# Attention and a mixture of experts on one core: the experts' second product with tokens as the stationary side

## The chip, the cores and the metric

The kernel runs on one core of a Trainium2 chip. The metric is device microseconds of one execution. TensorE (PE in the profile, PEld for its weight loads) multiplies a stationary operand of up to 128 columns with a moving operand and writes PSUM; VectorE (DVE) and ScalarE (ACT) read PSUM and copy; GpSimd (POOL) issues the gathers and scatters; SyncE (SP) issues the weight loads.

## The reference

Attention of 4 batches, 8 heads, 576 tokens, 64 features with a position bias; its output, as 2304 rows of 512, goes through eight experts, one per token:

```
logits = x @ w_gate;  e_idx = argmax(logits)
gate_w = softmax(logits)[e_idx];  eom = sigmoid(x @ w_output_gate)
for e in range(8):                       # N, D, E, F = 2304, 512, 8, 1024
    mask = e_idx == e
    h = np.maximum(x[mask] @ w1[e], 0.0) # 512 -> 1024
    ye = h @ w2[e]                       # 1024 -> 512
    out[mask] = gate_w[mask, None] * eom[mask, e, None] * ye
```

All is fp32.

## The kernel before

The attention comes first and scales its rows by the two gates; they go to `x_dram`. A router on DVE sorts the tokens into slots of `CH = 288` tokens of one expert (or of 96, a small slot). `gidx` holds the rows to gather and `sidx` the rows of the answer to scatter to, both 96 to a column, so that a slot has three columns. The routing is done in two parts, the second of them piecewise during slots 0 to 2 (`SLOT_WORK`).

With these inputs eight full slots run through `body(s)`, s = 0 to 7, and then one `small(8)`; slots from 4 on stand in a branch on a flag (`either`). Precision is kept by splitting: each operand becomes a high and a low part in fp32r, and three products (high by high, high by low, low by high) are summed in PSUM. `split(hi, lo, src)` is a cast on ACT and a subtraction on DVE.

`body(s)` has two stages.

- Stage 1, L1029 to L1044: for each of eight blocks f of 128 hidden units, twelve matmuls (L1035), weights stationary, 288 token columns moving. ACT writes `hh[f]` (L1037), DVE `hl[f]` (L1038). At even f the pair `w2r[f//2]` is split (L418, L419).
- Stage 2, L1050 to L1078: for each of four blocks d of 128 outputs, 24 matmuls (L1056), w2 stationary, 288 tokens moving. The result has outputs on partitions, so ACT copies it to `yt` (L1062) and twelve transposes (L1073) turn it into three blocks of 96 tokens; DVE, ACT and DVE copy these to `y` (L1076), and POOL scatters them (L1001). Between the blocks d, `w1r[d]` of the next slot is split and the next slot's tokens are transposed (L439 to L441).

Engines run their queues in program order. SP loads w2 of slot s+1 into `w2r` (L415) when stage 1 has split the old one, and w1 of slot s+2 into `w1r` (L410) when stage 2 has. PSUM has three buffers for `p1`, two for `p2` and three for `pt`.

Of the kernel before, what the change touches and what calls it, by code (L numbers as in the profile page):

```python
# [9 lines left out]
F32 = mybir.dt.float32  # L10
# [122 lines left out]
def attention_moe_kernel(  # L133
# [15 lines left out]
    nc = tc.nc  # L149
    V = nc.vector  # L150
# [32 lines left out]
    def psum_t():  # L183
        return ps_t.tile([128, 512], F32, name="pt", tag="t")
# [45 lines left out]
    gidx = [const.tile([G, NG], U32, name=f"gidx{i}") for i in range(2)]  # L230
    sidx = [const.tile([G, NG], U32, name=f"sidx{i}") for i in range(2)]
    ids_a = const.tile([G, NG], F32, name="ids_a")
# [11 lines left out]
    def route_group(part):  # L244
# [153 lines left out]
        V.scalar_tensor_tensor(out=fi, in0=ids, scalar=-1.0, in1=fi, op0=ALU.add, op1=ALU.add)  # L398
        V.tensor_copy(out=sidx[part][:, 0:ng], in_=fi)


    w1r, w1h, w1l, w2r, xs, xg = [], [], [], [], {}, {}

# [44 lines left out]
    def first_x():  # L448
        t = nat.tile([G, 2, DM], F32, name="xg0", tag="nat")
        t1 = biasp.tile([G, 4, DM], F32, name="xg1", tag="bias4")  # L450
        xg[0] = [t[:, 0, :], t[:, 1, :], t1[:, 3, :]]
        xg[1] = [t1[:, j, :] for j in range(3)]
        gather(0)
# [531 lines left out]
    with ExitStack() as ctx:  # L985
# [8 lines left out]
        hh, hl = ([t[:, i, :] for i in range(8)] for t in (hh_all, hl_all))  # L994
        yts = [qx.tile([128, 4, CH], F32, name=f"yt{t}", tag=t) for t in ("qt1", "qs1")]

        puts = []

        def put(s, j, y):
            idx = sidx[int(s >= SURE_A)][:, 3 * s + j:3 * s + j + 1]  # L1000
            p = nc.gpsimd.indirect_dma_start(  # L1001
                out=out, out_offset=bass.IndirectOffsetOnAxis(ap=idx, axis=0),
                in_=y, in_offset=None, bounds_check=NTOK - 1, oob_is_err=False,
            )
            for other in puts:
                tc.declare_no_dep(p.ins, other.ins, reason="no row of the answer is written twice")
            puts.append(p)

        y2 = vp.tile([G, DM], F32, name="y2", tag="v")

        def new_y(s, j):

            if s == SURE:
                return xg[1][j]
            return y2 if j == 2 else x_p.tile([128, DM], F32, name="y", tag="x")[0:G]

# [5 lines left out]
        def ahead(s):  # L1022

            return s <= SURE

        def body(s):
            assert s < BIG or not (work or rows)
            xh, xl = xs[side(s)]
            for f in range(8):  # L1029
# [14 lines left out]
                slot_work(s, "f%d" % f)  # L1044
            if ahead(s + 1):
                load_w2(s + 1)
            if ahead(s + 2):
                gather(s + 2)
            yt = yts[s % 2]
            for d in range(4):  # L1050
                ds = slice(d * 128, d * 128 + 128)
                p2 = ps2.tile([128, 512], F32, name="p2", tag="p2")
                n = 0
                for f in range(8):
                    for w, x in ((w2h, hh), (w2h, hl), (w2l, hh)):
                        nc.tensor.matmul(  # L1056
                            p2[:, 0:CH], lhsT=w[f // 2][:, f % 2, ds], rhs=x[f], start=n == 0, stop=n == 23
                        )
                        n += 1
                if ahead(s + 1):  # L1060
                    split(w1h[d], w1l[d], w1r[d])
                nc.scalar.copy(out=yt[:, d, :], in_=p2[:, 0:CH])  # L1062
                if ahead(s + 1) and d in (1, 2):
                    for c in (2 * d - 2, 2 * d - 1):
                        transpose_x(s + 1, c)
                slot_work(s, "d%d" % d)
            if ahead(s + 2):
                load_w1(s + 2)
            pts = [psum_t() for j in range(3)]
            for d0, d1 in ((0, 3), (3, 4)):  # L1070
                for j, pt in enumerate(pts):
                    for d in range(d0, d1):
                        nc.tensor.transpose(pt[0:G, d * 128:d * 128 + 128], yt[:, d, j * G:j * G + G], ident)  # L1073
            for j, pt in enumerate(pts):
                y = new_y(s, j)
                (V.tensor_copy, nc.scalar.copy, V.tensor_copy)[j](out=y, in_=pt[0:G, :])  # L1076
                if s != SURE:
                    put(s, j, y)  # L1078

        def small(s):  # L1080
# [3 lines left out]
            xh, xl = xs[side(s)]  # L1084
            h = yts[s % 2].rearrange("p a b -> p (a b)")[0:G, 0:DFF]
            for i in range(2):
# [42 lines left out]
            y = new_y(s, 0)  # L1129
            nc.scalar.copy(out=y, in_=p2[0:G, :])  # L1130
            if s != SURE:
                put(s, 0, y)

# [25 lines left out]
        for j in range(3):  # L1159
            put(SURE, j, xg[1][j])  # L1160

# [28 lines left out]
```

## Time and profile before

| what | value |
|---|---|
| three timed runs | 638.07, 639.40, 639.48 us; median 639.4 |
| profiled execution | 638.0 us, span 636.1 us |
| PE busy | 589.8 us, 93% of the span |
| DVE, ACT, POOL busy | 428.9, 386.9, 86.1 us |
| chain that ended last | PE 78%, DVE 10%, DMA 3%, ACT 3%, issue 3% |
| lines with the most of it | PE L1056 16%, PE L1035 15%, PE L844 13% |
| granted clock | 0.984 over the span |

The chain of work that ended last is followed back from the last instruction; its shares say which engine's work set the end. Matmuls overlap in the pipeline, so their busy time is not their cost: the cost of one is the distance from its start to the next start. The experts begin at about 380 us of the span; the full slots end at 613 us.

### The profile page before, as it was taken

Reading aid. Unit: us, or ns where it says so; the run is one execution under the profiler, and the core shown is the slowest. Engines: PE = TensorE matmul, PEld = TensorE weight load, DVE = VectorE, ACT = ScalarE, POOL = GpSimd, SP = SyncE. Lnnn points to the kernel's source line nnn. Section 1 sums busy time; section 2 is a strip of 40 time slices with the busy share of each in tenths; the row PEclk is TensorE's granted clock in tenths of the full one; section 3 lists DMA queues with packets and bytes.
Section 4 is the critical chain, followed back from the end, with each engine's and each line's share of the span. In section 5 each row is a group of like instructions: output and inputs, shape, how many; then the busy total and the mean of one; then the engine's idle time right before and its main releaser. Section 6 shows DMA issues by size and latency. Waiting matters only on the chain.

```text
span 636.1 us, 13589 instructions
## 1 busy us (share of the span) xinstructions
PE 589.8 (93%) x5036; PEld 497.8 (78%) x5036; DVE 428.9 (67%) x1011; ACT 386.9 (61%) x785; POOL 86.1 (14%) x140
## 2 busy tenths in 40 slices
PE   4878889999999999999998789999999999999993
PEld 2323578877888888877786659999999999999982
DVE  6968766667787778765897457687755465564651
ACT  5778777777777777677655634454545354554551
POOL 1000000000000000000000470040322304041011
PEclk9979999999999999999999899999999999999997
DMA  6989975665557655773564755555657556565510
GB/s 144 223 190 213 219 158 121 132 141 126 111 125 184 140 122 127 176 162 74 118 158 134 247 175 158 195 174 166 204 163 248 166 178 200 175 205 179 158 40 8
DMA packets 99387, 100.73 MB, mean 158 GB/s; under 512 B 71511, under 2 KB 71767, under 8 KB 99304
## 3 DMA queue, kind: packets, MB, share of 16 engines
q1 hardware_dynamic: 93028, 84.93, 52.6%
q0 software_dynamic: 3520, 10.03, 5.1%
q10 hardware_dynamic: 2756, 4.72, 2.1%
q8 instruction: 45, 0.74, 0.5%
q14 instruction: 38, 0.31, 0.1%
HBM read 60.73 MB, written 10.03 MB: 111 GB/s over the span
## 4 chain that ended last, share of the span: by engine, by line
PE 78%; DVE 10%; DMA 3%; ACT 3%; issue 3%; SPq 0%; POOLq 0%; POOL 0%; DVEq 0%; ACTq 0%
PE p L1056 16%; PE p L1035 15%; PE pa L844 13%; PE pt L812 10%; PE ps L775 9%; DVE hid L642 3%; PE pb L653 3%; PE ps L791 3%; PE pt L725 2%; DVE e L755 2%; PE pt L1073 2%; PE pt L439 2%; PE pt L824 1%; PE pt L577 1%; DMA kl<-qs 1%
## 5 line engine op out<-in xcount | busy, mean ns | idle before, releaser
L760 ACT ACTIVATE e<-e,nm 128x576 f32<-128x576 f32 x144 | 111.6, 776 | 52.8 <-DVE nm L755 51.5
L755 DVE CUSTOM_DVE_ANT_0 e<-ps,bias 128x576 f32<-128x576 f32 x144 | 106.0, 753 | 35.1 <-PE ps L775 29.5
L1035 PE MATMUL p<-x,w 128*128 128x288 f32 x768 | 107.9, 300 | 1.1 <-issue 0.6
L1035 PEld LDWEIGHTS p<-x,w 128*128 128x128 f32 x768 | 104.4, 191 | 2.5 <-issue 1.4
L812 PE MATMUL pt<-kept,e 128*128 128x128 f32 x576 | 83.1, 279 | 1.7 <-ACT e L760 0.7
L775 PE MATMUL ps<-qt,qs 128*128 128x288 f32 x256 | 79.3, 328 | 3.1 <-DVE nm L755 2.3
L812 PEld LDWEIGHTS pt<-kept,e 128*128 128x128 f32 x576 | 66.1, 142 | 16.1 <-issue 7.4
L1056 PE MATMUL p<-hh,w2h 128*128 128x288 f32 x256 | 77.0, 301 | 0.0
L1056 PE MATMUL p<-hl,w2h 128*128 128x288 f32 x256 | 75.7, 296 | 0.8 <-DVE hl L1038 0.8
L1056 PE MATMUL p<-hh,w2l 128*128 128x288 f32 x256 | 75.5, 295 | 0.7 <-DVE w2l L419 0.7
L844 PE MATMUL pa<-et,vt 128*64 128x256 f32 (+1 forms) x640 | 73.2, 354 | 2.1 <-ACT xt L845 2.0
L775 PE MATMUL ps<-kl,qs 128*128 128x288 f32 x256 | 70.7, 294 | 0.0
L816 ACT COPY et<-pt 128x512 f32<-128x512 f32 x103 | 57.4, 578 | 12.9 <-PE pt L812 12.7
L653 PE MATMUL pb<-hid,w2blk 128*32 128x288 f32 x576 | 48.4, 442 | 17.6 <-DVE hid L642 7.7
L844 PEld LDWEIGHTS pa<-et,vt 128*64 128x64 f32 x640 | 42.6, 137 | 24.2 <-issue 5.5
L1037 ACT ACTIVATE hh<-p 128x288 fp32r<-128x288 f32 x64 | 26.2, 412 | 49.2 <-PE p L1035 41.6
L775 PEld LDWEIGHTS ps<-qt,qs 128*128 128x128 f32 x256 | 48.3, 189 | 7.1 <-DVE nm L755 3.9
L419 DVE TENSOR_TENSOR w2l<-w2r,w2h 128x1024 fp32r<-128x1024 f32 x36 | 44.0, 1224 | 13.9 <-ACT w2h L418 12.3
L642 DVE TENSOR_SCALAR hid<-e,early 128x576 f32<-128x576 f32 x110 | 48.5, 516 | 7.1 <-PE pb L653 3.7
L653 PEld LDWEIGHTS pb<-hid,w2blk 128*32 128x32 f32 x576 | 19.1, 115 | 43.0 <-DVE hid L642 11.2
L1001 POOL DMA_INDIRECT out_dram<-y,sidx x24 | 26.4, 1098 | 183.9 <-DVE y L1076 179.1
L419 DVE TENSOR_TENSOR w<-w1r,w 128x1024 fp32r<-128x1024 f32 x32 | 39.2, 1224 | 17.3 <-ACT w L418 17.2
(189 smaller groups left out, 1014.6 us busy)
## 6 DMA issues: line engine op xcount, KB each, us to landing
w1r<-in_moe_w_dram SPq DMA_DIRECT2D x36, 512.0 KB, 4.2
w2r<-in_moe_w_dram SPq DMA_DIRECT2D x36, 512.0 KB, 3.5
kl<-qs SPq DMA_DIRECT2D x32, 288.0 KB, 5.3
nat<-in_k_dram SPq DMA_DIRECT2D x16, 288.0 KB, 3.5
nat<-in_q_dram SPq DMA_DIRECT2D x16, 288.0 KB, 6.0
bias<-evh SPq DMA_DIRECT2D x16, 288.0 KB, 4.5
bias<-evl SPq DMA_DIRECT2D x16, 288.0 KB, 5.0
qs<-qt SPq DMA_DIRECT2D x16, 288.0 KB, 3.2
```

What stands on the lines that cost most here:

```text
L419: V.tensor_tensor(out=lo, in0=src, in1=hi.bitcast(F32), op=ALU.subtract)
L642: V.tensor_scalar(out=to, in0=src, scalar1=bc[:, r:r + 1], scalar2=0.0, op0=ALU.add, op1=ALU.max,)
L653: nc.tensor.matmul(pb[32 * t:32 * t + 32, c, 0:288], lhsT=w2f, rhs=hids[t][:, c * 288:c * 288 + 288], start=True, stop=True,)
L755: V.tensor_tensor_reduce(out=e.rearrange("p (a j) -> p a j", a=2), in0=ps[:, :, 0:n], in1=bias_ap.rearrange("p (a j) -> p a j", a=2), scal ...
L760: nc.scalar.activation(out=e, in_=e, func=ACTF.Exp, scale=-1.0, bias=nm, accum_out=sum_ap)
L775: nc.tensor.matmul(ps[:, c, 0:288], lhsT=qs[:, o:o + 128], rhs=keys[:, k0 + c * 288:k0 + c * 288 + 288], start=n == 0, stop=n == 1,)
L812: nc.tensor.transpose(pt[:, n * 256 + j * 128:n * 256 + j * 128 + 128], es[j][:, (n0 + n) * 128:(n0 + n) * 128 + 128], ident,)
L816: copy(out=et[:, n0:n0 + nn, :].rearrange("p n s -> p (n s)"), in_=pt[:, 0:nn * 256])
L844: nc.tensor.matmul(pa[p:p + 64, 0:n], lhsT=values, rhs=weights, start=i == 0, stop=i == 4)
L1001: p = nc.gpsimd.indirect_dma_start(out=out, out_offset=bass.IndirectOffsetOnAxis(ap=idx, axis=0), in_=y, in_offset=None, bounds_check=NTOK ...
L1035: nc.tensor.matmul(p1[:, 0:CH], lhsT=w[:, fs], rhs=x[:, c, :], start=n == 0, stop=n == 11)
L1056: nc.tensor.matmul(p2[:, 0:CH], lhsT=w[f // 2][:, f % 2, ds], rhs=x[f], start=n == 0, stop=n == 23)
```

## The change

`hh` and `hl` become the stationary side and w2 the moving one, so the product comes out with tokens on partitions and outputs along the row. The 288 tokens are taken in blocks of 128, 128 and 32. The first two blocks take the three split products, 24 matmuls of 512 columns each, in two halves of twelve (`half`). The third (`rest`) is in plain fp32: POOL adds `hh` and `hl` of its 32 tokens to `hr`, and 32 matmuls multiply it with the unsplit `w2r`, 128 output columns at a time on four groups of 32 array columns. The twelve transposes and the `yt` copies are gone; two 128x512 copies and four of 32x128 take results from PSUM to `y`. The load of the next w2 is issued behind `rest`. The scatter index `sidx` has a column of 128, 128 and 32 tokens, filled by six small copies instead of one. The scatters are issued in the order block 2, block 0, block 1.

```diff
-    sidx = [const.tile([G, NG], U32, name=f"sidx{i}") for i in range(2)]
+    sidx = [const.tile([128, 3, NSLOT], U32, name=f"sidx{i}") for i in range(2)]
...
-        V.tensor_copy(out=sidx[part][:, 0:ng], in_=fi)
-
-
-    w1r, w1h, w1l, w2r, xs, xg = [], [], [], [], {}, {}
+        fi = fi.rearrange("p (s j) -> p j s", j=3)
+        for j in range(3):
+            n = 0
+            while n < min(128, CH - 128 * j):
+                g, p = divmod(128 * j + n, G)
+                m = min(G - p, CH - 128 * j - n, 128 - n, 128 if n == p == 0 else 64 if p % 64 == n % 64 == 0 else 32)
+                V.tensor_copy(out=sidx[part][n:n + m, j, 0:ng // 3], in_=fi[p:p + m, g, :])
+                n += m
...
-        t1 = biasp.tile([G, 4, DM], F32, name="xg1", tag="bias4")
-        xg[0] = [t[:, 0, :], t[:, 1, :], t1[:, 3, :]]
-        xg[1] = [t1[:, j, :] for j in range(3)]
+        t1 = biasp.tile([128, 4, DM], F32, name="xg1", tag="bias4")
+        xg[0] = [t[:, 0, :], t[:, 1, :], t1[0:G, 3, :]]
+        xg[1] = [t1[0:G, j, :] for j in range(3)]
+        late.extend(t1[:, j, :] for j in range(3))
...
-        yts = [qx.tile([128, 4, CH], F32, name=f"yt{t}", tag=t) for t in ("qt1", "qs1")]
-
+        hts = [qx.tile([128, 4, CH], F32, name=f"ht{t}", tag=t) for t in ("qt1", "qs1")]
+        blocks = (slice(0, 128), slice(128, 256), slice(256, CH))
+
+        nc.gpsimd.memset(late[0][G:128], 0.0)
+        nc.gpsimd.memset(late[1][G:128], 0.0)
...
-            idx = sidx[int(s >= SURE_A)][:, 3 * s + j:3 * s + j + 1]
+        def put(s, j, y, n=None):
+            n = n or y.shape[0]
+            idx = sidx[int(s >= SURE_A)][0:n, j, s:s + 1]
             p = nc.gpsimd.indirect_dma_start(
                 out=out, out_offset=bass.IndirectOffsetOnAxis(ap=idx, axis=0),
-                in_=y, in_offset=None, bounds_check=NTOK - 1, oob_is_err=False,
+                in_=y[0:n], in_offset=None, bounds_check=NTOK - 1, oob_is_err=False,
...
-        y2 = vp.tile([G, DM], F32, name="y2", tag="v")
+        y2 = vp.tile([CH - 256, DM], F32, name="y2", tag="v")
...
-            if ahead(s + 1):
-                load_w2(s + 1)
+            hr = hts[s % 2].rearrange("p a b -> p (a b)")[:, 0:256].rearrange("p (f t) -> p f t", f=8)
+            for i in range(2):
+                fs = slice(i * 4, i * 4 + 4)
+                nc.gpsimd.tensor_tensor(
+                    out=hr[:, fs, :], in0=hh_all[:, fs, blocks[2]].bitcast(F32),
+                    in1=hl_all[:, fs, blocks[2]].bitcast(F32), op=ALU.add,
+                )
             if ahead(s + 2):
                 gather(s + 2)
-            yt = yts[s % 2]
-            for d in range(4):
-                ds = slice(d * 128, d * 128 + 128)
-                p2 = ps2.tile([128, 512], F32, name="p2", tag="p2")
-                n = 0
-                for f in range(8):
+            p2s = [None] * 3
+
+            def half(j, i):
+                if i == 0:
+                    p2s[j] = ps2.tile([128, 512], F32, name="p2", tag="p2")
+                n = 12 * i
+                for f in range(4 * i, 4 * i + 4):
                     for w, x in ((w2h, hh), (w2h, hl), (w2l, hh)):
                         nc.tensor.matmul(
-                            p2[:, 0:CH], lhsT=w[f // 2][:, f % 2, ds], rhs=x[f], start=n == 0, stop=n == 23
+                            p2s[j], lhsT=x[f][:, blocks[j]], rhs=w[f // 2][:, f % 2, :], start=n == 0, stop=n == 23
                         )
                         n += 1
+
+            def rest():
+                p2s[2] = psum_t()
+                for f in range(8):
+                    for g in range(4):
+                        nc.tensor.matmul(
+                            p2s[2][32 * g:32 * g + 32, 0:128], lhsT=hr[:, f, :],
+                            rhs=w2r[f // 2][:, f % 2, g * 128:g * 128 + 128], start=f == 0, stop=f == 7,
+                        )
+                if ahead(s + 1):
+                    load_w2(s + 1)
+
+            def answer(j):
+                y = new_y(s, j)
+                if j < 2:
+                    (nc.scalar.copy, V.tensor_copy)[j](out=y, in_=p2s[j])
+                else:
+                    for g, copy in enumerate((V.tensor_copy, nc.scalar.copy) * 2):
+                        copy(out=y[:, g * 128:g * 128 + 128], in_=p2s[2][32 * g:32 * g + 32, 0:128])
+                if s != SURE:
+                    put(s, j, y)
+
+            def next_x(cs):
+                for c in cs if ahead(s + 1) else ():
+                    transpose_x(s + 1, c)
+
+            steps = (
+                (lambda: half(0, 0), rest),
+                (lambda: half(0, 1), lambda: answer(2), lambda: next_x((0, 1))),
+                (lambda: half(1, 0), lambda: answer(0), lambda: next_x((2, 3))),
+                (lambda: half(1, 1), lambda: answer(1)),
+            )
+            for d in range(4):
+                for step in steps[d]:
+                    step()
                 if ahead(s + 1):
                     split(w1h[d], w1l[d], w1r[d])
-                nc.scalar.copy(out=yt[:, d, :], in_=p2[:, 0:CH])
-                if ahead(s + 1) and d in (1, 2):
-                    for c in (2 * d - 2, 2 * d - 1):
-                        transpose_x(s + 1, c)
                 slot_work(s, "d%d" % d)
             if ahead(s + 2):
                 load_w1(s + 2)
-            pts = [psum_t() for j in range(3)]
-            for d0, d1 in ((0, 3), (3, 4)):
-                for j, pt in enumerate(pts):
-                    for d in range(d0, d1):
-                        nc.tensor.transpose(pt[0:G, d * 128:d * 128 + 128], yt[:, d, j * G:j * G + G], ident)
-            for j, pt in enumerate(pts):
-                y = new_y(s, j)
-                (V.tensor_copy, nc.scalar.copy, V.tensor_copy)[j](out=y, in_=pt[0:G, :])
-                if s != SURE:
-                    put(s, j, y)
...
-            put(SURE, j, xg[1][j])
+            put(SURE, j, late[j][0:(128, 128, CH - 256)[j]])
```

On DVE, at the end of slot 3 (`w_1` is the low part of w1, `x` the next slot's tokens, `y` a result row block). Before:

```order
L419 TENSOR_TENSOR w_1_4598<-w1r_4426,w_0_4597 128x1024
L441 TENSOR_TENSOR x<-pt,x 128x288 x2
L419 TENSOR_TENSOR w_1_4598<-w1r_4427,w_0_4597 128x1024
L441 TENSOR_TENSOR x<-pt,x 128x288 x2
L419 TENSOR_TENSOR w_1_4598<-w1r_4428,w_0_4597 128x1024
L1076 COPY y<-pt 96x512
L1076 COPY y_4892<-pt 96x512
```

and now:

```order
L426 TENSOR_TENSOR w_1_4603<-w1r_4425,w_0_4602 128x1024
L1097 COPY y_4899<-pt 32x128 x2
L448 TENSOR_TENSOR x<-pt,x 128x288 x2
L426 TENSOR_TENSOR w_1_4603<-w1r_4426,w_0_4602 128x1024
L448 TENSOR_TENSOR x<-pt,x 128x288 x2
L426 TENSOR_TENSOR w_1_4603<-w1r_4427,w_0_4602 128x1024
L1094 COPY y<-p_6164 128x512
L426 TENSOR_TENSOR w_1_4603<-w1r_4428,w_0_4602 128x1024
```

The last split of w1 (`w1r_4428`) stood ahead of the copies of `y`; it now stands behind one.

On PE, where slot 2 ends and slot 3 begins. Before:

```order
L1056 MATMUL p_5946<-hh,w2h_4883 128x288
L1056 MATMUL p_5946<-hl,w2h_4883 128x288
L1056 MATMUL p_5946<-hh,w2l_4887 128x288
L1073 MATMUL pt<-kept,ytqt_4890 96x128 x12
L1035 MATMUL p_6017<-x,w_0_4597 128x288 x2
L1035 MATMUL p_6017<-x,w_1_4598 128x288
```

and now, in the middle of slot 2's stage 2, where `rest` stands between the halves of block 0:

```order
L1075 MATMUL p_5776<-w2h_4886,hh 128x512
L1075 MATMUL p_5776<-w2h_4886,hl 128x512
L1075 MATMUL p_5776<-w2l_4890,hh 128x512
L1084 MATMUL pt<-w2r,htqt_4895 32x128 x32
L1075 MATMUL p_5776<-w2h_4887,hh 128x512
```

The twelve transposes at the slot's end are gone, and 32 narrow matmuls stand behind the first twelve wide ones.

On POOL, one slot (`xg` gathers, `out_dram` scatters, `htqs` holds `hr`). Before:

```order
L1001 DMA out_dram<-y,sidx_104 2304x512 x2
L1001 DMA out_dram<-y_4892,sidx_104 2304x512
L429 DMA xg_4650<-x_dram,gidx_102 96x512 x3
L1001 DMA out_dram<-y,sidx_104 2304x512 x2
L1001 DMA out_dram<-y_4892,sidx_104 2304x512
```

and now:

```order
L1061 TENSOR_TENSOR htqs_4896<-hh,hl 128x128 x2
L436 DMA xg_4655<-x_dram,gidx_102 96x512 x3
L1013 DMA out_dram<-y_4899,sidx_104 2304x512
L1013 DMA out_dram<-y,sidx_104 2304x512 x2
L1061 TENSOR_TENSOR htqt_4895<-hh,hl 128x128 x2
```

The two adds stand ahead of the gathers of slot s+2, which so wait for the end of stage 1.

## Rows read from the trace of the kernel before

**Rows 1.** Span and mean granted clock of the core.
```profile
core 0: 636.1 us, clock 0.984
```
**Rows 2.** Chain that ended last, slots 0 and 5: start us, us, what, count.
```profile
396.46 6.41 PE p L1056 x48
...
541.90 6.40 PE p L1056 x48
548.30 0.50 PE pt L439 x6
548.80 3.22 PE p L1056 x24
...
555.74 1.31 PE pt L1073 x12
557.05 12.92 PE p L1035 x96
```
**Rows 3.** Stage 2 of slot 5: length; PE, PEld, DVE, ACT, POOL busy; clock, DMA, GB/s.
```profile
541.90:557.00 15.10, 15.10 (x122) 14.98 (x120) 8.09 (x11) 7.00 (x13) 0.00 (x0) 1.00 0.57 180
```
**Rows 4.** Matmuls of 512 columns in the small slot, by form, then by time.
```profile
L1094 PE MATMUL p<-w,x 128*96 128x512 f32 x24 | 5.8, 395 | 0.4 <-issue 0.4
```
```profile
613.66 5.76 PE L1094 MATMUL p<-w,x 128*96 128x512 f32 x24 [0.35 <-issue]
```
**Rows 5.** Plain fp32 matmuls on groups of array columns: chain, then by time.
```profile
371.28 2.38 PE pa L844 x20
```
```profile
139.62 0.29 PE L775 MATMUL ps<-kl,qs 128*128 128x288 f32 x1
139.85 0.64 PE L508 MATMUL pt<-xt,wgb 128*32 128x256 f32 x8
140.42 0.66 PE L812 MATMUL pt<-kept,e 128*128 128x128 f32 x4
```
**Rows 6.** Groups by form: line, operation, count, then busy us, mean ns, idle before.
```profile
L419 DVE TENSOR_TENSOR w<-w1r,w 128x1024 fp32r<-128x1024 f32 x32 | 39.2, 1224 | 17.3 <-ACT w L418 17.2
...
L827 DVE COPY et<-pt 128x512 f32<-128x512 f32 x16 | 11.0, 687 | 0.3 <-PE pt L824 0.3
...
L462 POOL TENSOR_TENSOR w<-w1r,w 128x512 fp32r<-128x512 f32 x8 | 10.1, 1278 | 12.9 <-ACT w L461 12.8
...
L744 POOL CAST q<-qs 128x128 fp32r<-128x128 f32 x16 | 4.6, 290 | 33.7 <-DMA qs<-qt 33.6
...
L827 DVE COPY et<-pt 64x128 f32<-64x128 f32 x16 | 4.4, 273 | 1.2 <-PE pt L824 1.2
```
**Rows 7.** PE and DVE by time, slot 1: a low part awaited by PE.
```profile
427.71 1.20 DVE L419 TENSOR_TENSOR w2l<-w2r,w2h 128x1024 fp32r<-128x1024 f32 x1
...
428.97 0.40 PE L1056 MATMUL p<-hh,w2l 128*128 128x288 f32 x1 [0.74 <-DVE w2l L419]
...
429.21 0.30 PE L1056 MATMUL p<-hh,w2h 128*128 128x288 f32 x1
...
430.10 0.40 PE L1056 MATMUL p<-hl,w2h 128*128 128x288 f32 x1 [0.59 <-DVE hl L1038]
```
**Rows 8.** DVE by time around the end of stage 1 of slot 0.
```profile
398.05 0.69 DVE L582 TENSOR_TENSOR x<-pt,rec 128x512 f32<-128x512 f32 x1 [1.41 <-DMA x_dram<-x]
398.66 0.45 DVE L1038 SCALAR_TENSOR_TENSOR hl<-p,hh 128x288 fp32r<-128x288 f32 x1
```
**Rows 9.** SP's w2 load during slot 5 by time; then its issues: KB, us to landing.
```profile
533.43 9.91 SPq L415 DMA_DIRECT2D w2r<-in_moe_w_dram  x4
```
```profile
w2r<-in_moe_w_dram SPq DMA_DIRECT2D x4, 512.0 KB, 3.5
```
**Rows 10.** DVE by time at the first scatter index.
```profile
354.79 0.18 DVE L399 CAST sidx<-fi 96x39 uint32<-96x39 f32 x1
356.94 0.76 DVE L755 CUSTOM_DVE_ANT_0 e<-ps,bias 128x576 f32<-128x576 f32 x1 [1.97 <-PE ps L791]
```
**Rows 11.** The last scatter on POOL.
```profile
629.74 0.92 POOL L1001 DMA_INDIRECT out_dram<-xg,sidx  x1 [0.30 <-issue]
```

More of the change, by code (lines that the diff above doesn't have):

```diff
@@ L398, in route_group @@
         V.scalar_tensor_tensor(out=fi, in0=ids, scalar=-1.0, in1=fi, op0=ALU.add, op1=ALU.add)
-        V.tensor_copy(out=sidx[part][:, 0:ng], in_=fi)
-    w1r, w1h, w1l, w2r, xs, xg = [], [], [], [], {}, {}
+        fi = fi.rearrange("p (s j) -> p j s", j=3)
[6 more added lines that the diff above has]
+                n += m
+    w1r, w1h, w1l, w2r, xs, xg, late = [], [], [], [], {}, {}, []
     def expert(s):
@@ L994, in attention_moe_kernel @@
         hh, hl = ([t[:, i, :] for i in range(8)] for t in (hh_all, hl_all))
-        yts = [qx.tile([128, 4, CH], F32, name=f"yt{t}", tag=t) for t in ("qt1", "qs1")]
+        hts = [qx.tile([128, 4, CH], F32, name=f"ht{t}", tag=t) for t in ("qt1", "qs1")]
+        blocks = (slice(0, 128), slice(128, 256), slice(256, CH))
+        nc.gpsimd.memset(late[0][G:128], 0.0)
+        nc.gpsimd.memset(late[1][G:128], 0.0)
         puts = []
-        def put(s, j, y):
-            idx = sidx[int(s >= SURE_A)][:, 3 * s + j:3 * s + j + 1]
+        def put(s, j, y, n=None):
+            n = n or y.shape[0]
+            idx = sidx[int(s >= SURE_A)][0:n, j, s:s + 1]
             p = nc.gpsimd.indirect_dma_start(
                 out=out, out_offset=bass.IndirectOffsetOnAxis(ap=idx, axis=0),
-                in_=y, in_offset=None, bounds_check=NTOK - 1, oob_is_err=False,
+                in_=y[0:n], in_offset=None, bounds_check=NTOK - 1, oob_is_err=False,
             )
@@ L1007, in put @@
             puts.append(p)
-        y2 = vp.tile([G, DM], F32, name="y2", tag="v")
+        y2 = vp.tile([CH - 256, DM], F32, name="y2", tag="v")
         def new_y(s, j):
+            n = blocks[j].stop - blocks[j].start
             if s == SURE:
-                return xg[1][j]
-            return y2 if j == 2 else x_p.tile([128, DM], F32, name="y", tag="x")[0:G]
+                return late[j][0:n]
+            return y2 if j == 2 else x_p.tile([128, DM], F32, name="y", tag="x")
         def slot_work(s, at):
@@ L1084, in small @@
             xh, xl = xs[side(s)]
-            h = yts[s % 2].rearrange("p a b -> p (a b)")[0:G, 0:DFF]
+            h = hts[s % 2].rearrange("p a b -> p (a b)")[0:G, 0:DFF]
             for i in range(2):
@@ L1129, in small @@
             y = new_y(s, 0)
-            nc.scalar.copy(out=y, in_=p2[0:G, :])
+            nc.scalar.copy(out=y[0:G], in_=p2[0:G, :])
             if s != SURE:
-                put(s, 0, y)
+                put(s, 0, y, G)
         def either(s):
```

## The prediction

> **What bounds the kernel now.** I read the page first: PE is busy 93% of the span and the chain that ended last is 78% PE, with L1056, the line that changes, as its largest part at 16%. Then the chain in order of time through the experts: in slot 5 it goes from L1056 to the transposes of x to L1056 again, to the twelve transposes L1073 and on to L1035 of the next slot, with no other engine in it [rows 2]. The reader is to see that stage 2 is a sum of PE pieces: 6.40 + 3.22 + 3.22 us of L1056, two times 0.50 of L439, 1.31 of L1073 (the second 3.22 and 0.50 are like the first). The busy times of that stretch say the same from the other side: of 15.10 us PE has all, DVE 8.09, ACT 7.00, POOL none, at the full granted clock of 2.4 GHz [rows 3]. So a microsecond taken from PE here is a microsecond of the end, as long as no other engine takes its place. The exception is slot 1, where the routing on DVE is late and PE waits for `w2l` and `hl` [rows 7].
>
> **The sum on PE.** Removed from each full slot: 96 matmuls L1056, 12.84 us, and 12 transposes, 1.31, together 14.15 us [rows 2]. Added: 48 matmuls of 512 columns and 32 narrow ones.
>
> The 512-column matmul in fp32r is in the trace with 96 stationary columns instead of 128: 24 of them took 5.76 us, one lasts 0.395, so the distance from start to start is (5.76 - 0.395) / 23 = 0.2333 us [rows 4]. That is the value taken. From below it is bounded by 512 columns at one a cycle of 2.4 GHz, 0.2133; from above by the 288-column pitch scaled, 3.22 / 24 x 512 / 288 = 0.2385 [rows 2]. 48 x 0.2333 = 11.20 us.
>
> The narrow ones: plain fp32 on groups of columns. Twenty of 256 columns on two groups took 2.38 us, so a pair costs 0.238 us [rows 5]. Eight of 256 columns on four groups run from 139.85 to the next line at 140.42, 0.57 us [rows 5]; two sets of four at 0.238 are 0.476, and what is left, about 0.09, is the change of form. The same shows ahead of them: the matmul before started at 139.62, its follower was due 0.13 later, and it came at 139.85, again 0.09 late. So four groups cost what two do, and the price goes with the columns: 128 of them, 0.119 for a set of four. Eight sets and two changes: 8 x 0.119 + 0.19 = 1.14 us. Bounds: 0.85 (eight times 128 columns at two cycles, no change of form) and 2.28 (four times 0.57, as if half the columns cost the same). I take 1.14, since both rows of [rows 5] agree on it.
>
> The Trainium skill speaks against this part in TensorEngine Tiling, Key Properties: a change of the tiling mode drains TensorE. [Rows 5] show 0.09 us on either side, with the first narrow matmul starting before the 0.29 us of the one ahead were over; by the rule a wide matmul would have to end first, 0.395 instead of 0.233, in and out 0.32 instead of 0.19, and the sum would be 1.0 us worse over eight slots.
>
> New stage 2: 11.20 + 1.14 = 12.34, against 14.15: -1.81 us a slot, -14.5 over eight.
>
> **What comes back: a wait at seven slot boundaries, +5.5.** The last DVE work of stage 2 used to be the copies of `y`, and the low part of `w1r[3]` stood ahead of them. Now the copy of block 1 stands ahead of that low part, and it waits for the last matmul of the slot. Call E the moment when the next slot's first matmul is due. The last wide matmul started 0.233 before E and lasts 0.395, so it ends at E + 0.16; the copy starts about 0.05 later, a 128x512 copy from PSUM on DVE takes 0.69 [rows 6], and the low part 1.22 [rows 6]: done at E + 2.1. PE gets it 0.06 later, as in slot 1, where the DVE instruction ended at 428.91 and PE started at 428.97 [rows 7]. In L1035's order that low part is wanted by the twelfth matmul, 11 x 0.1346 = 1.48 after E (12.92 / 96 [rows 2]). The wait is 0.68, and the matmul behind a wait follows at 0.24 instead of 0.13 [rows 7]: 0.79 us. Behind the waiting copy on DVE stand only this low part and then `hl[0]`, which is not wanted before block 3. It falls between full slots, seven times; the small slot wants the same part after ten matmuls of 0.233 and does not wait. 7 x 0.79 = 5.5.
>
> **Slots 0 and 1, +0.7.** `rest` starts 12 x 0.233 = 2.80 us into stage 2 and needs the POOL add, which needs `hl[7]`. In slot 0 DVE first waits for the store of a row block and ends `hl[7]` at 399.11, which is 2.65 into stage 2 [rows 2, 8]. The add is not in the trace: a POOL cast of 128x128 took 0.29 and a POOL subtraction of 128x512 took 1.28 [rows 6], a quarter of which is 0.32. I take 0.35, near the cast, which has the add's size; with two hand-overs `hr` is there at 3.1, a wait of 0.3 (bound 1.2). In slot 1 PE has waited for the last `hl` until 430.10 [rows 7] with most of stage 2 still to do; now it will have done half of block 0 by then, wait for the add as well, and I estimate that it saves some 0.4 us less than the other slots. In the other slots `hl[7]` comes after one instruction of ACT and one of DVE, the latter 0.45 [rows 8], about 1 us into stage 2, and even 1.28 us of add hide behind the first half; were both adds to wait for `hl[7]` at that price, it would be 0.8 a slot.
>
> **Costed at nothing.** The copies: ACT and DVE lose four 288-column copies, three of `y`, and get two of 128x512 and four of 32x128 (a 64x128 one took 0.27 [rows 6]); both idle for half of stage 2 [rows 3]. The low part of `w1r[2]` and the x parts end before E by the same clock. The gathers of slot s+2 move some 12 us later on POOL, behind the adds; they are wanted a whole slot later. The w2 load: SP used to issue its four parts during stage 1 as the splits freed them, 9.91 us from first to last [rows 9]; now all four are issued about 4 us into stage 2, and the w1 loads behind them on SP. The first is wanted some 11 us later, the last 21; each lands in 3.5 [rows 9], 14 for all four even one after another. The five extra index copies: 5 x 0.18 = 0.9 us on DVE; the first time DVE idles 1.97 behind them [rows 10], the second time they lie in slot 2's stage 1. Without that cover 0.9 each. The tail: the last three scatters took 0.92 each with 96 rows [rows 11] and now have 128, 128 and 32, between -0.6 and +0.6 us; I take none.
>
> **The sum.** -14.5 + 5.5 + 0.7 = -8.3 us. The profiled execution took 638.0 us (span 636.1 [rows 1] and 1.9 around it), so it becomes 629.7. It lies at the low end of the three timed runs, whose median is 639.4; by the median the forecast is 631.1 us.
>
> **Rivals.**
>
> - Narrow matmuls dearer. If a set of four takes four cycles a column, it costs 0.213, `rest` 8 x 0.213 + 0.19 = 1.90, and the time is 8 x 0.76 = 6.1 us higher: 637.2. Against it stands the pair of 256 columns at 0.238, where four cycles would be 0.427 [rows 5]. The Trainium skill says so in FP8 and Floating Point Precision, TensorE Precision Notes: true fp32 makes four passes through the array; the trace does not agree. Other costs between 1.14 and 2.28 end in the same region, 634 to 638.
> - The boundary wait doesn't show, because DVE gets to the low part in time or the pitch is nearer 0.213 with the same effect: 631.1 - 5.5 = 625.6. For it, DVE has half of stage 2 idle [rows 3]; against it, the queue is in order and the copy cannot start before E + 0.2.
> - Slower: the four groups don't overlap when all load the same `hr`. Then 32 matmuls at the price of a transpose of 128 columns, 1.31 / 12 = 0.109 [rows 2], are 3.49 + 0.19 = 3.68 us, 2.54 more a slot, 20.3 in all: 651.4. It decides once `rest` passes 1.14 + 8.3 / 8 = 2.2 us. Against it: the eight matmuls in 0.57 us [rows 5].
> - The change doesn't do what it says, since the wide pitch is at its upper bound and `rest` waits for POOL in every slot: 384 x 0.0052 + 6.4 = +8.4, 639.5, no change.
>
> **How the numbers follow.** Forecast 631.1 with its own range 628.5 to 633.5: 0.55. Boundary wait hidden or shorter, 624 to 628.5: 0.13. `rest` dearer or more waiting, 633.5 to 637.5: 0.20. No change: 0.05. Slower: 0.07. A measurement of this kernel can tell about 0.3%, 2 us, from no change. Faster by more than that: 0.88; within: 0.05; slower: 0.07. The range for 8 in 10 is 625.5 to 637.5: it takes in most of both neighbours and leaves out the slower case.
>
> **What would show it.** In the changed profile: L1075 at about 0.233 us from start to start, and a stage 2 of some 13.3 us with the transposes of x; L1084, 32 matmuls, in about 1.1 us; L1048 with a wait of about 0.8 us once a slot for the DVE low part at L426, and DVE waiting for PE at L1094 just before. Wrong if L1084 takes over 2 us, if PE waits for POOL at L1061 in the later slots, if ACT waits for a DMA at the w2 split, or if the granted clock falls behind the waits.

## The result: 0.6% slower where 1.3% faster was forecast

The changed kernel took 643.26 us, median of 6 runs (642.21 to 644.64); the kernel before, run beside it on the same chip, took 639.84, median of 6 (638.07 to 640.77). The ratio is 1.0057, 95% interval [1.0041, 1.0074]. The profiled execution took 643.61 us, with a span of 641.8 against 636.1 [rows 1].

The chain that ended last, by time through the beginning of stage 2 in slots 3 and 4 of the changed kernel (start us, us, what, count). It answers to the chain of slot 5 in [rows 2]:

```profile
488.61 2.79 PE p L1075 x12
491.40 1.89 PE pt L1084 x64
493.29 2.98 PE p L1075 x12
...
516.39 2.79 PE p L1075 x12
519.18 2.08 PE pt L1084 x54
521.26 0.29 issue
521.55 0.44 PE pt L1084 x6
521.99 0.29 issue
522.28 0.43 PE pt L1084 x4
522.71 3.15 PE p L1075 x12
```

Two things are to be seen. Even where it runs through, the narrow part L1084 is 1.89 us and not 0.95, and it has 64 records where the program has 32 matmuls. And in slot 4 it lasts 3.53 us (522.71 - 519.18), cut by two stops under "issue", which is time in which PE waits for nothing that the profile shows. Slots 0, 5 and 6 look like slot 4, slot 7 like slot 3; in slots 1 and 2 the narrow part waits for POOL in its middle.

The boundary between slots 4 and 5, the same view, and then the group of stage 1 over all slots (busy us, mean ns, idle before and its releaser):

```profile
529.66 2.82 PE p L1075 x12
532.49 0.02 issue
532.51 0.06 DVE y L1094
...
533.12 1.23 DVE w L426
534.34 0.04 issue
534.39 0.66 PE p L1048 x3
```
```profile
L1048 PE MATMUL p<-x,w 128*128 128x288 f32 x768 | 108.0, 299 | 3.8 <-DVE w L426 3.8
```

The path leaves PE at the end of the slot, goes over the copy of block 1 and the low part of `w1r[3]` behind it on DVE, and comes back to the twelfth matmul of stage 1, as forecast.

Stage lengths, from the starts of the first matmuls of each stage on PE by time (us). The first column is the stretch from the first wide matmul of slot 0 to the first of the small slot. Before this stretch no changed matmul runs; it starts at 396.2 and 395.9 in the two executions of before and between 394.2 and 398.7 in the four of the changed kernel, so stretches are compared, not ends.

| execution | stretch | stage 1 of slots 1 to 7 | stage 2 of 0 to 7 | stage 2: slot 0 | 1 | 3 | 4 | 5 | 6 |
|---|---|---|---|---|---|---|---|---|---|
| before | 217.4 | 92.4 | 125.1 | 15.83 | 17.41 | 15.52 | 15.17 | 15.17 | 15.29 |
| after | 222.0 | 95.6 | 126.3 | 17.01 | 17.92 | 14.27 | 16.08 | 16.16 | 16.03 |
| before again (e10) | 215.8 | 90.7 | 125.1 | 15.81 | 17.40 | 15.52 | 15.23 | 15.17 | 15.29 |
| after again (e5) | 213.0 | 95.6 | 117.3 | 15.04 | 16.35 | 14.28 | 14.28 | 14.28 | 14.28 |
| after, third (e9) | 214.5 | 95.6 | 118.9 | 15.04 | 17.91 | 14.27 | 14.28 | 14.28 | 14.28 |
| after, fourth (e11) | 222.3 | 96.0 | 126.3 | 17.04 | 16.34 | 14.27 | 16.65 | 16.59 | 16.59 |

So of +4.5 us in the stretch, +3.3 stand in stage 1 and +1.2 in stage 2, which was to lose 13.8.

### The profile page after: what moved, and what is told of

The parts are those of the page before. It is cut to its first block, busy times and chain, and to the rows that moved or that the text cites. A ratio compares the mean times of both kernels' runs of the same rounds, so it can differ in the third digit from the quotient of the medians.

```text
span 641.8 us, 13731 instructions
## 1 busy us (share of the span) xinstructions
PE 587.8 (92%) x5068; PEld 470.9 (73%) x5068; DVE 429.1 (67%) x1029; ACT 378.6 (59%) x769; POOL 102.2 (16%) x158
## 4 chain that ended last, share of the span: by engine, by line
PE 68%; DVE 10%; DMA 10%; issue 5%; ACT 4%; POOL 1%; SPq 0%; POOLq 0%; DVEq 0%; ACTq 0%
PE pa L852 13%; PE p L1048 10%; PE p L1075 10%; PE pt L820 9%; PE ps L783 9%; DMA out_dram<-y,sidx 6%; PE pb L661 4%; PE ps L799 3%; PE pt L733 2%; DMA bias<-evh 2%; PE pt L1084 2%; DVE e L763 2%; PE pt L585 1%; PE pt L832 1%; DVE w L426 1%
## 5 line engine op out<-in xcount | busy, mean ns | idle before, releaser
L1048 PE MATMUL p<-x,w 128*128 128x288 f32 x768 | 108.0, 299 | 3.8 <-DVE w L426 3.8
L1048 PEld LDWEIGHTS p<-x,w 128*128 128x128 f32 x768 | 104.8, 190 | 6.1 <-DVE w L426 5.4
L852 PE MATMUL pa<-et,vt 128*64 128x256 f32 (+1 forms) x640 | 74.8, 360 | 2.1 <-ACT xt L853 2.0
L1075 PE MATMUL p<-w2h,hh 128*128 128x512 f32 x128 | 53.5, 418 | 0.1
L426 DVE TENSOR_TENSOR w2l<-w2r,w2h 128x1024 fp32r<-128x1024 f32 x36 | 43.9, 1222 | 12.2 <-ACT w2h L425 12.1
L1075 PE MATMUL p<-w2l,hh 128*128 128x512 f32 x128 | 51.3, 401 | 0.0
L1075 PE MATMUL p<-w2h,hl 128*128 128x512 f32 x128 | 51.1, 399 | 0.0
L783 PEld LDWEIGHTS ps<-kl,qs 128*128 128x128 f32 x256 | 48.6, 190 | 0.0
L426 DVE TENSOR_TENSOR w<-w1r,w 128x1024 fp32r<-128x1024 f32 x32 | 39.3, 1228 | 7.4 <-ACT w L425 7.3
```

Of the source, the lines that this page charges most:

```text
L426: V.tensor_tensor(out=lo, in0=src, in1=hi.bitcast(F32), op=ALU.subtract)
L783: nc.tensor.matmul(ps[:, c, 0:288], lhsT=qs[:, o:o + 128], rhs=keys[:, k0 + c * 288:k0 + c * 288 + 288], start=n == 0, stop=n == 1,)
L852: nc.tensor.matmul(pa[p:p + 64, 0:n], lhsT=values, rhs=weights, start=i == 0, stop=i == 4)
L1048: nc.tensor.matmul(p1[:, 0:CH], lhsT=w[:, fs], rhs=x[:, c, :], start=n == 0, stop=n == 11)
L1075: nc.tensor.matmul(p2s[j], lhsT=x[f][:, blocks[j]], rhs=w[f // 2][:, f % 2, :], start=n == 0, stop=n == 23)
```

## Experiments

e1 to e4 ran on one chip, e5 to e8 on a second, e9 and e10 on a third, e11 and e12 on a fourth. Times are compared on one chip. Which chip the first comparison had is not on record; it can be that of e11.

**What the narrow part costs (e3).** Half of its matmuls are left out, so the third block is summed over half of the hidden units only.

```
-                for f in range(8):
+                for f in (0, 2, 4, 7):
```

> The change with half of the third block's sum left out (hidden blocks 0, 2, 4 and 7 of eight), 16 narrow matmuls a slot instead of 32. Theory (each plain fp32 matmul runs as two records, 64 a slot at about 0.03 us): 32 records a slot, 1.08 us instead of 1.9 to 3.5, and the time falls by 8 x 0.85 = 7 us or, if the idle stretches go with them, 11 to 14. Rival (32 narrow matmuls at 1.14 us as predicted, the loss is elsewhere): falls by 8 x 0.5 = 4 us.

Ratio 0.986 [0.9838, 0.9883], 627.44 us. That is 6.0 us less than e2 below, the nearest to the changed kernel on the same chip, and the stages 2 add up to 6.1 less. The chain in slot 4:

```profile
507.89 2.32 PE p L1075 x10
510.21 1.01 PE pt L1084 x32
511.22 2.99 PE p L1075 x12
```

32 records instead of 64, 1.01 us instead of 1.89; a plain stage 2 takes 13.40 instead of 14.27. A set of four (eight records) costs 0.88 / 4 = 0.22 us. What doesn't go with the number is the 0.13 left here and the 0.19 by which the next wide part is longer (2.98 for 2.79), 0.32 us together. The forecast had 0.119 for a set. The reading that gave it can be checked in the trace of before, in the summary of the line that it was taken from:

```profile
L508 PE MATMUL pt<-xt,wgb x96: 219/379/404, 139.8 to 378.1; 128*32 128x256 f32 x64, 128*32 128x64 f32 x32
```

The program has 48 matmuls there, the trace 96. Each plain fp32 matmul stands as two records. The eight records that took 0.57 us [rows 5] were four matmuls, one set and not two. The other row has the same fault: the program has 480 matmuls in L844 and the trace 960 records, so the twenty in 2.38 us are ten matmuls, and a pair costs 0.476 us and not 0.238.

**The gathers ahead of the POOL adds (e2).** They go back into stage 1, where the kernel before has them.

```
+            if ahead(s + 2):
+                gather(s + 2)
             for i in range(2):
                 ... hr = hh + hl on POOL
-            if ahead(s + 2):
-                gather(s + 2)
```

> The change, with the gathers of slot s+2 issued on POOL ahead of the two adds, as before the change. Theory G (PE's idle stretches of 0.3 us inside L1084 in slots 0 and 4 to 6 come from the gathers that POOL issues at the same time): they go, L1084 takes 1.9 us in every slot instead of 3.5 to 3.9, and the time falls by 5 to 7 us. Rival F (PE runs short of instructions by itself, since 64 loads and 64 matmuls pass in 1.9 us): the idle stretches stay, and the time is within 1.5 us of the changed kernel.

Ratio 0.9952 [0.9931, 0.9974], 633.43 us; no stop in any slot, a plain stage 2 of 14.28. That looked like a gain of 1% over the changed kernel, but the two had run on different chips, and the next run took the comparison away.

**The changed kernel again (e5, e9).** No edit.

> The changed kernel again, for what its gaps hang on. In its trace the narrow matmuls L1084 of slots 0, 4, 5 and 6 are cut by stops of 0.29 to 0.33 us that no wait explains (3.5 to 3.9 us instead of 1.89), and in none of the four variants run so far. Theory A (they belong to the program: this order of instructions brings them in each execution): the same slots show them again, the sum over slots of stage 2 is 126 us, the ratio 1.005 to 1.007. Theory B (they belong to an execution): they stand in other slots or not at all in this profile, and the time spreads by several us between executions or lies near 0.995.

Ratio 0.9959 [0.9937, 0.998], 633.25 us against 636.09. The chain in slot 4:

```profile
509.69 2.79 PE p L1075 x12
512.48 1.88 PE pt L1084 x64
514.37 2.75 PE p L1075 x11
```

> The changed kernel a third time: the first comparison gave 1.0057 [1.0041, 1.0074], with stops in L1084 in slots 0, 4, 5 and 6; the second 0.9959 [0.9937, 0.998], with none. Theory B1 (the stops belong to one loading or one chip, and the change without them is worth -2 to -3 us): L1084 x64 in 1.89 us in slots 0 and 3 to 7, stage 2 117 to 119 us, ratio 0.994 to 0.998. Theory B2 (they come and go from one loading to the next): stops again, perhaps in other slots, 126 us, ratio near 1.005; or something between.

On another chip 0.9971 [0.9945, 0.9996], 633.3 against 635.48, and again no stop. The same program is thus 0.3 to 0.4% faster than before on two chips and 0.6% slower in the first comparison.

**Before again (e10).**

> The kernel before, unchanged, for a trace of it beside the last one. Ratio 1.000 within 0.002, a bound for what two copies of one program differ by on one chip. If the first trace of before holds stops of the same kind too, stage 2 of slots 3 and 7 (15.52 and 15.67 there, 15.17 in slots 4 and 5) comes out at 15.17 here and its start of the experts moves from 379.7; if the stops belong to the narrow matmuls of the change alone, the stages are as they were within 0.2 us.

Ratio 1.0003 [0.9983, 1.0024]. Stage 2 is as in the first trace within 0.1 us in every slot, 15.52 in slot 3 included, so stage 2 of before has no stops in either trace. Stage 1 of slots 2 and 4 took 1.6 us more, together, the first time. There the first trace of before shows something that e10 does not. ACT starts `hh` 0.04 to 0.10 us after the last matmul of its block ends, in every slot of e10 from slot 1 on; in the first trace it is 1.3 to 2.7 us late at three blocks each of slots 2 and 4, those that end while POOL issues the gathers or just after. In slot 4 the third block ends on PE at 504.68, the three gathers are issued from 503.93 to 507.47, and PE then waits for a free PSUM buffer, until the DVE part behind this `hh` ends at 508.26 (ACT and PE by time):

```profile
507.35 0.41 ACT L1037 ACTIVATE hh<-p 128x288 fp32r<-128x288 f32 x1 [3.77 <-PE p L1035]
```
```profile
508.31 1.85 PE L1035 MATMUL p<-x,w 128*128 128x288 f32 x12 [0.43 <-issue]
```

The kernel before is itself slower where there are stops: 639.8 us in the first comparison and 639.7 beside e11, against 635.5 to 636.1 on the other three chips. The 1.6 us are a part of these 4; the rest was not followed up.

**The changed kernel and the gathers' place on one chip (e11, e12).** No edit in e11; e12 has that of e2.

> The changed kernel a fourth time, to find the stops in L1084 of the first comparison once more (they were in none of the profiles on three other chips). Theory G (they need two things, gathers on POOL beside L1084 and a chip or a loading of that kind): where they come, they come in slots 0, 4, 5 and 6 together, with a ratio near 1.005, and not in slot 7, which has no gathers. Theory B1 (they were of that one loading): none, ratio 0.994 to 0.999.

> The order with the gathers ahead of the POOL adds again, beside the changed kernel on one chip: the first time it had 0.9952 [0.9931, 0.9974] on another chip than the changed kernel's 1.0057. Theory B1: where the changed kernel has no stops, moving the gathers is worth nothing, the two ratios agree within 0.003. Theory G: if the changed kernel shows stops here, this one shows them as well (its gathers lie beside L1084 too) or, with the gathers 1.4 us earlier, fewer of them.

Here the stops were back. e11: 1.004 [1.0013, 1.0067], 643.23 us against 639.74 of before, nearly the two medians of the first comparison. e12 on the same chip: 0.9922 [0.9894, 0.9949], 634.58 us. Slot 4 in the chain of e11, and then of e12:

```profile
519.37 1.65 PE pt L1084 x50
...
521.05 0.44 PE pt L1084 x4
521.49 0.32 issue
521.80 0.44 PE pt L1084 x6
522.24 0.32 issue
522.56 0.43 PE pt L1084 x4
```
```profile
512.55 2.79 PE p L1075 x12
515.35 1.88 PE pt L1084 x64
517.23 2.99 PE p L1075 x12
```

Stage 2 adds up to 126.3 us in e11 and 117.3 in e12; the 9.0 between them are 2.0 in slot 0 and 2.3 each in slots 4 to 6, and the times differ by 8.65. So moving the gathers away takes the stops of L1084 with it. In e11 a further stop follows among the wide matmuls behind L1084, 0.38 us in L1075 in each of slots 4 to 6. The stops need at least two things: gathers beside L1084, and a chip of this kind or a loading of this kind; the runs don't part these two. They come in slots 0, 4, 5 and 6 together and never in slot 7, which has no gathers, as the theory of the gathers had it. One part of its expectation for e12 was wrong: it put e12's gathers beside L1084 too, and they lie in stage 1.

What they do can be placed to a tenth of a microsecond. POOL by time in slot 4 of the changed kernel's first trace, then PE's weight loads in the same stretch (start us, us, engine, line; in brackets the idle time ahead):

```profile
518.01 1.40 POOL L1061 TENSOR_TENSOR htqt<-hh,hl 128x128 f32<-128x128 f32 x1 [5.93 <-DVE hl L1051]
519.56 0.95 POOL L436 DMA_INDIRECT xg<-x_dram,gidx  x1 [0.15 <-issue]
520.82 0.92 POOL L436 DMA_INDIRECT xg<-x_dram,gidx  x1 [0.30 <-issue]
522.04 0.91 POOL L436 DMA_INDIRECT xg<-x_dram,gidx  x1 [0.30 <-issue]
```
```profile
519.11 1.45 PEld L1084 LDWEIGHTS pt<-w2r,htqt 128*32 128x32 f32 x51 [0.37 <-issue]
520.84 0.15 PEld L1084 LDWEIGHTS pt<-w2r,htqt 128*32 128x32 f32 x4 [0.28 <-issue]
521.56 0.17 PEld L1084 LDWEIGHTS pt<-w2r,htqt 128*32 128x32 f32 x6 [0.56 <-issue]
522.29 0.15 PEld L1084 LDWEIGHTS pt<-w2r,htqt 128*32 128x32 f32 x3 [0.56 <-issue]
```

The weight loads run at full rate for one gather, stop at 520.56, 0.05 us after it ends, and then come in groups of 4, 6 and 3 with 0.28 to 0.56 us between them while the second and third gather follow. Two rivals can be settled from the traces. A late fetch of instructions isn't seen: from 511 to 527 us the instruction queues moved no packet, in the view of the DMA queues. The load of the next w2 begins in this stretch too, 0.95 us after L1084 does, but in e12 it begins 0.63 us after L1084 and nothing stops. On the other chips the gathers stand just as close, without a stop; in e5:

```profile
512.86 0.95 POOL L436 DMA_INDIRECT xg<-x_dram,gidx  x1 [0.15 <-issue]
```

And slot 3 has gathers beside L1084 on every chip and no stop on any; its first gather runs beside DVE's low part L426 and takes 1.61 us instead of 0.95. Yet slot 3 is not untouched. DVE's first copy of block 2, which waits for PE's signal from L1084, comes 2.5 us after the end of L1084 (493.29) in the first trace, and 0.07 us after it (486.58) in e5:

```profile
495.76 0.28 DVE L1097 COPY y<-pt 32x128 f32<-32x128 f32 x1 [3.99 <-remote]
```
```profile
486.65 0.28 DVE L1097 COPY y<-pt 32x128 f32<-32x128 f32 x1 [1.59 <-PE pt L1084]
```

In the first trace and e11 this copy is 1.3 us late in slots 4 to 6, 2.5 to 3.5 in slots 1 to 3, and not late in slot 7, which has no gathers; in e5, e9 and e12 it comes 0.07 us after L1084 in every slot but slot 1 (0.69). The semaphore events of the trace say the same of slot 3: PE's four signals from L1084 lie 0.44 us apart in e5, and the last comes 2.4 us late in the first trace. So where there are stops, PE's results are also handed on late beside the gathers, in the first trace of before too (at e10), and both lie in the same stretches. The ends of matmuls in a profile are modelled, so whether PE finishes late or only its signal comes late, and how chips differ in it, no run here shows.

**The copy of block 1 on ACT (e1).**

```
-                    (nc.scalar.copy, V.tensor_copy)[j](out=y, in_=p2s[j])
+                    (V.tensor_copy, nc.scalar.copy)[j](out=y, in_=p2s[j])
```

> The change, with block 1's copy on ACT and block 0's on DVE. Theory (boundary wait): the low part of w1r[3] no longer stands behind the copy on DVE; L1048's waits for L426, 3.8 to 5.4 us at seven boundaries in the changed kernel, go to under 1, and the time falls by 4 to 5 us, to 638 to 639. Rival (the wait is only moved, to ACT, whose copy then delays hh[0], or the time is set elsewhere): within 1.5 us of the changed kernel, 643.

Ratio 1.0052 [1.0032, 1.0072], 639.68 us, without stops. That is 6.2 us more than e2 on the same chip, and stage 1 of slots 1 to 7 is 6.5 longer. The wait only moved, and grew, as the rival had it; that the time lies near the 638 to 639 of the theory comes from the chip. In the chain at the end of slot 4 the copy on ACT now stands ahead of ACT's cast of `w1r[3]`, and the DVE part follows that:

```profile
531.28 0.04 ACT y L1094
...
531.76 1.06 ACT w L425
532.82 0.02 issue
532.84 1.24 DVE w L426
```

L1048 waits 8.4 us in all instead of 3.8, and stage 1 takes 14.5 instead of 13.5.

**The narrow part after the second half of block 0 (e4).**

```
-                (lambda: half(0, 0), rest),
-                (lambda: half(0, 1), lambda: answer(2), lambda: next_x((0, 1))),
-                (lambda: half(1, 0), lambda: answer(0), lambda: next_x((2, 3))),
+                (lambda: half(0, 0),),
+                (lambda: half(0, 1), rest, lambda: next_x((0, 1))),
+                (lambda: half(1, 0), lambda: answer(2), lambda: answer(0), lambda: next_x((2, 3))),
```

> The change, with the narrow matmuls behind both halves of block 0 instead of between them. Theory (in slots 0 to 2 PE waits for the POOL add, and in slot 1 the granted clock falls to 0.70 behind that wait): PE's wait for L1061 goes from 4.3 us to under 0.5, the clock in slot 1's stage 2 stays at 1.00, the time falls by 3 to 4 us. Rival (slot 1 is bound by DVE's hl[7] anyway, which the second half of block 0 needs too): the wait moves to L1075 <- DVE, the clock falls all the same, and the time is within 1.5 us.

Ratio 1.0043 [1.0024, 1.0062], 638.26 us. Stage 2 gains: 14.53 in slot 1 instead of 16.35 to 17.92, since the POOL add is done by then. Stage 1 gives more back: 8.0 us more than in e2 on the same chip, against 3.2 less in stage 2. All copies now follow late, so the splits behind them do too, and the group of stage 1 says what PE waits for:

```profile
L1048 PE MATMUL p<-x,w 128*128 128x288 f32 x768 | 110.6, 300 | 7.9 <-DVE w L426 7.2
```

**The low part ahead of the copy (e6, e7, e8).** The last split of a slot is written ahead of `answer(1)`:

```
-                (lambda: half(1, 1), lambda: answer(1)),
+                (lambda: half(1, 1),),
             ...
                 if ahead(s + 1):
                     split(w1h[d], w1l[d], w1r[d])
+                if d == 3:
+                    answer(1)
```

> The changed kernel with one edit: at the end of a slot the low part of w1r[3] comes before the copy of block 1 on DVE. It undoes the wait at the boundary alone. Theory: stage 1 falls from 13.51 to 12.89 us in seven slots, -4.3 us, ratio 1.0057 - 0.0068 = 0.999 if the stops in L1084 stay. Rival 1 (another instruction takes the place of the wait, as with the copy on ACT): stage 1 stays at 13.5, ratio 1.0057. Rival 2 (the stops go as well, as in the four variants): another -7 us, ratio 0.988.

e6 took 628.76 us beside 633.25 of the unchanged e5 on the same chip, 4.5 us less; ratio to before 0.9893 [0.9864, 0.9921]. Stage 1 of slots 1 to 7 falls from 95.6 to 92.2 us, 3.5 of the 4.3 expected: 12.78 in slots 1, 3 and 4, but 13.26 in slots 5 to 7. There PE still stands behind the eleventh matmul, now until the copy of block 1 is done (PE by time, the beginning of slot 5):

```profile
521.63 1.64 PE L1048 MATMUL p<-x,w 128*128 128x288 f32 x11
523.47 2.79 PE L1048 MATMUL p<-x,w 128*128 128x288 f32 x19 [0.20 <-DVE y L1094]
```

The low part of `w1r[3]`, which the twelfth wants, ended at 522.81 us, the copy at 523.41; this costs half a microsecond. These are the slots that follow one in the branch on a flag. Why PE waits for the copy there was not followed up.

> The order of e6 and the gathers ahead of the POOL adds (as in e2, ratio 0.9952). Theory: the two gains add up, stage 1 12.89 and stage 2 14.27 in the later slots, ratio 0.9952 - 0.0068 = 0.988. Rival (what e2 gained is partly the same time, since a PE that does not wait at the boundary reaches L1084 before the POOL add is done): L1084 waits for POOL in the later slots by some 0.3 to 0.6 us, ratio 0.992 to 0.995.

e7 adds the edit of e2: 0.9889 [0.9852, 0.9925], 628.01 us, the same as e6 within the intervals. On a chip without stops the place of the gathers is worth nothing that these runs can show.

e8 has, besides, e4's order in slots 0 to 2 alone, with `answer(2)` right behind the narrow part:

```
-                (lambda: half(0, 0), rest),
-                (lambda: half(0, 1), lambda: answer(2), lambda: next_x((0, 1))),
+                (lambda: half(0, 0),) if s < 3 else (lambda: half(0, 0), rest),
+                (lambda: half(0, 1), *((rest,) if s < 3 else ()), lambda: answer(2), lambda: next_x((0, 1))),
```

> As e7, and in slots 0 to 2 the narrow matmuls come after the second half of block 0 instead of the first, so that the POOL add has 2.8 us more. Theory: slot 1 loses its wait for POOL (1.9 us) and the stretch at a granted clock of 0.70 behind it (1.7 us), slot 0 its 0.8; -3 to -4 us against e7, ratio 0.983. Rival (the clock falls in slot 1 because PE has idled before, for the late routing, and not for this wait): only the wait goes, -1 to -2 us, or nothing, if the copies of block 2 then come too late: ratio 0.985 to 0.988.

0.9862 [0.9836, 0.9887], 626.91 us, the fastest of all that compute the whole answer, though its interval overlaps those of e6 and e7. Slot 1's stage 2 falls from 16.38 to 14.53, slot 2's from 14.78 to 14.20, and slot 0 gives back 0.85; in all -1.6 us in the stretch, where -3 to -4 were expected, since the stretch at a lower clock was not there in e7 either. These three were not run on a chip that shows the stops; e7 and e8 have the gathers at the place at which e12 had no stops.

## Why the prediction was wrong, by its steps

**The wide matmuls: right.** 0.2333 us from start to start was taken; twelve of slot 6 run from 575.48 to 578.04, 2.56 / 11 = 0.2327.

**The narrow matmuls: mis-sized, and the largest error that holds on every chip.** The step "two sets of four at 0.238 are 0.476" took records for matmuls. `rest` costs 1.89 + 0.19 = 2.08 us and not 1.14: 0.94 in each of eight slots, 7.5 us. By e3, 0.81 of the 0.94 are the sets, 0.22 each instead of 0.119, and 0.13 the change of form, 0.32 instead of 0.19. A plain slot 5 goes from 15.17 to 14.28, -0.89, where -1.81 was forecast and -0.87 follows with this one term set right.

It was the first rival, at 1.90 and 637.2 us, that is 0.9966 of its median; e5 and e9 measured 0.9959 and 0.9971. That it comes so close is in part luck: `rest` is 0.18 dearer still, 1.4 us in all, and the shorter boundary wait gives 1.2 back. What stood against it, the pair at 0.238, was the same misreading.

The Trainium skill had it, in FP8 and Floating Point Precision, TensorE Precision Notes: true fp32 takes four passes. An estimate from that, four cycles for each of 128 columns at 2.4 GHz, is 0.213 us a set. The trace agrees with that page, with 0.22; the forecast's sentence that it does not came from the misreading. The Trainium skill also states, in TensorEngine Tiling, Key Properties, that a change of the tiling mode drains TensorE; the forecast worked out 0.32 us from it and took 0.19, and e3 leaves 0.32. That this time is a drain no run here shows.

**The wait at the boundary: right in kind, a fifth too large.** 0.60 to 0.65 us in six of seven slots against 0.79, PE waiting for L426 behind L1094; e6 takes most of it away, 3.5 us of stage 1, and the medians of e5 and e6 differ by 4.5.

**The gathers, "costed at nothing": the step that decided the sign where there are stops.** The forecast asked only when their result is wanted, a whole slot later. It did not ask what they run beside. Moved behind the adds they lie beside the narrow matmuls, and this costs 1.8 to 2.0 us in each of four slots in the first comparison and 2.0 to 2.4 in e11. The trace of before could not show the price, since there POOL does nothing at all in that stretch [rows 3]. It had one sign, which the prediction did not use: in stage 1 of slots 2 and 4 ACT takes up blocks 1.3 to 2.7 us late beside the gathers (shown at e10). In the changed kernel the same stage of slot 5, in that view, is

```profile
545.80:562.00 16.20, 15.49 (x127) 11.86 (x126) 7.46 (x11) 6.60 (x12) 6.47 (x6) 1.00 0.69 229
```

with 6.47 us of POOL. A new neighbour was added and given no bounds. None of the rivals had it: the slower one, groups that don't overlap, is refuted by 64 records in 1.89 us.

**Slots 0 and 1: slot 1 missed.** Slot 0's wait of 0.3 did not come: its second add ended at 399.25 us and the narrow part began at 400.35. (The forecast also took 396.46 from the chain for the start of that stage; by time it is 396.22.) Slot 1 was to gain 1.4 and lost 0.5 in the first trace. The narrow part's second half waited for the add and the clock fell behind it; PE and POOL by time, then the wide matmuls after it in the view of busy times (PE, PEld, DVE, ACT, POOL, granted clock, DMA share, GB/s):

```profile
433.17 0.45 POOL L1061 TENSOR_TENSOR htqs<-hh,hl 128x128 f32<-128x128 f32 x1 [8.39 <-DVE cb L329]
...
433.68 1.08 PE L1084 MATMUL pt<-w2r,htqs 128*32 128x128 f32 x32 [1.87 <-POOL htqs L1061]
```
```profile
434.76:439.30 4.54, 4.54 (x15) 3.58 (x15) 1.34 (x5) 0.52 (x2) 2.34 (x4) 0.62 1.02 317
```

The add is behind `hl[7]`, which DVE ends late here. At a mean granted clock of 0.62, between its levels of 1.2 and 2.4 GHz, twelve wide matmuls took 4.54 us; those in the middle start 0.43 us apart. In e5 the same wait was followed by the full clock:

```profile
429.64:434.20 4.56, 4.56 (x24) 3.78 (x25) 2.07 (x7) 1.81 (x5) 2.86 (x4) 1.00 0.99 345
```

So the wait is the change's (it goes in e4 and e8), and the 1.6 us of lower clock behind it come in some executions: in the first, e9, e1 and e2, not in e5, e11 and e12.

**Added up** for the chips without stops: -8.3 forecast, +7.5 for `rest`, -1.2 for the shorter boundary wait, makes -2.0 us; measured -2.8 (633.25 against 636.09) and -2.2 (633.3 against 635.48). In the first comparison about 7 us of stops come on top (stage 2 of e9 against that of after: 118.9 and 126.3), which makes +5; the medians differ by 3.4, where the kernel before loses time of its own.

## What to carry to other kernels

Before a duration per instruction is read off the trace, hold the number of records against the number of instructions in the program. When a step is moved off an engine's path "because its result is wanted late", look at what it will run beside, and give that neighbourhood bounds of its own. And where a copy and a producer of the next stage stand on one in-order engine, write the producer first: here that was worth 3.5 us in the trace and 4.5 by the medians.

## What the hardware showed that was not expected

- One program can be 0.3 to 0.4% faster than another on two chips and 0.4 to 0.6% slower in two other comparisons, with intervals that don't touch (0.9959 [0.9937, 0.998] and 1.0057 [1.0041, 1.0074]). A comparison of two versions is one of the chip, or of the loading, that it was made on.
- Where indirect gathers are issued on POOL beside a dense run of narrow matmuls, PE can stop for 0.3 us at a time, for nothing that the profile names. In e11 wide matmuls stop so too, 0.38 us in L1075. In such stretches DVE or ACT gets PE's signal 1.3 to 3.5 us late, in both kernels.
- A POOL addition of 128x128 took 0.45 to 0.47 us alone or beside other DVE instructions, and 1.30 to 1.41 where it started 0.13 to 0.22 us behind DVE's low part L426 of the next weights. In slot 3 it started 0.16 us ahead of L426: it took 0.46, and L426, which had a gather beside it as well, 1.38 instead of 1.23. The summary of that line in the changed kernel, for the adds to one of the two buffers, has both (ns min/median/max, first and last start):

```profile
L1061 POOL TENSOR_TENSOR htqt<-hh,hl x8: 453/464/1402, 392.0 to 577.2; 128x128 f32<-128x128 f32 x8
```

The forecast took 0.35. From slot 3 on the long ones stayed hidden behind the first half of block 0; in slot 2 stage 2 took 0.3 us longer for one (14.56 against 14.28).
